# A static planner's urgencies, shifted class by class, in a fused RWKV-6 and MLP kernel

## The chip, the cores and the metric

The kernel runs on one core of one Trainium2 chip. The metric is the device time of one launch in microseconds (us), lower is better. The core has a matrix engine (PE, with its weight loads shown as PEld), a vector engine (DVE), a scalar engine (ACT), a general engine (POOL) and SyncE (SP), which here issues nearly all transfers. Each engine runs its own instructions in the order in which the program lists them.

## The reference

The first half is a linear attention with a decaying state. For each of 4 batches and 8 heads it walks over 768 steps of 48 channels:

```python
for t in range(S):
    cur = np.einsum('bhd,bhe->bhde', u[None] * kt, vt)
    y[:, :, t] = np.einsum('bhd,bhde->bhe', rt, state + cur)
    state = wt[:, :, :, None] * state + np.einsum('bhd,bhe->bhde', kt, vt)
```

The heads are laid side by side (8 x 48 = 384 features), and the second half is a normalised MLP of width 1536 with a residual:

```python
xn = (x - mu) / np.sqrt(var + 1e-06) * g_ln
ch = np.maximum(xn @ w_ch1, 0.0) @ w_ch2
return x + ch
```

## The kernel before

The 4 batches of 768 steps are cut into 8 **rounds** of 384 steps (half a batch each, all 8 heads), numbered 0 to 7. Round 0 is cut again into two **parts**, one of 128 steps and one of 256, so that the first results come early. A part goes through two stages of work.

The first is the scan, `front` (line 1539). Its inputs w, k, r are loaded (`load`, 474; `load_first` in round 0) and turned by PE (`turn`, 502: tiles `w_ps`, `k_ps`, `r_ps`). `totals` (547) multiplies decays pairwise, on DVE or POOL. Then six levels follow one another: `quads` (657) makes 96 small matmuls of 48 rows into a tile `a`, `grow` (689) multiplies k and r by the decays on DVE (tiles `k<-k,tot` and `r<-r,tot` in the profile), and `keep` (718) copies a masked part of the quads into a matrix A on DVE. After them come the transposed k (`kn_ps`), the `states` (860) with a scan on DVE (`s`), and the `outputs` (935). `load_v` (807) fetches v and a half-swapped copy `vx`. `own` makes the term of the current step (tiles `rk`, `vo`), on DVE or POOL.

The second is the MLP: `normalize` (1010) and `turn_x` make the normalised transposed input `xf`; then two products. Rounds 0 to 4 multiply the second product in plain float32 (tiles `o`), and round 0 the first product too (`h_ps<-xf,w`). Round 1 on, the first product is made in three pieces (`hd_ps` and twice `h_ps`), and in rounds 5 to 7 the second product is as well (`thirds`, 1316: nine matmuls for each of 12 slices f of the hidden layer, tiles `a` and `o_2`). The pieces of the weights are made on the way: `convert` (1141) turns 24 fetched blocks of weights into float32 (three ACT and two DVE instructions each), `halve` (1197) and `halve2` (1256) split them.

The small matmuls of `quads`, `states` and `outputs` use parts of the array; the planner calls them `tiled`, and the others not.

**What sets the order.** Nothing above is issued as it is written. Each piece is registered with `plan.add(engine, cost, function, reads, writes, ..., pri=...)`, and `Plan.order` (from line 112 on) then builds the order of every engine once, as the program is built: it keeps a modelled clock for each engine, and picks again and again the engine whose next piece can start first. Among the pieces of that engine that could start within `WAIT[engine]` of the earliest, the one with the lowest urgency number `pri` goes first. A piece that may run on `EITHER` engine (DVE or POOL) goes to the one that can start it first. Constants bend the model:

- `STAY` (in `switching`, 172) is added to the number of a PE piece that would change between tiled and untiled; `DRAIN` is the modelled time of such a change.
- `PATIENCE` (157) is how long, from the time it is ready, a POOL piece marked `port` is held back until DVE runs pieces not so marked.
- `MARGIN` takes the place of `HOP`, the modelled time from one engine to another, for tiled pieces once 60 us have passed (`FILLED`).
- `FETCH` is the modelled interval between fetches of PE's instructions.

Where PE would be idle for over 0.4 us in the first 90 modelled us, matmuls on a constant are put there (lines 192 to 199; tile `idle`).

The number is `at(rnd, stage) = 40 * rnd + stage` (409) for stages 0 to 30 of the scan and the normalisation. Part 0 of round 0 counts as round -1. `CONVERT` is 38. `FILL` is 200, so the MLP of round 0 has 200, of round 1 240, and so on to 320 and 360; rounds 5 to 7 have 400, 440 and 480 plus 2f for slice f, and 3 more for its `thirds`. Copies out of PSUM have `EVICT` = -1000, or a stage less 500.

Two shifts of the diff touch numbers that a reader would not guess: 14 is the fetch of the weights' blocks (`pri - 24`, line 1185; also the fourth `grow` of round 0), and 38 is all the conversions but DVE's share of the first six blocks and the fetches.

Since all pieces are recorded through one helper, every program line in the profile is L49; groups are told apart by their tiles.

Of the kernel before, what the change touches and what calls it, by code (L numbers as in the profile page):

```python
# [1 line left out]

# [63 lines left out]
class Plan:  # L66
# [11 lines left out]

    HOP, MARGIN, FILLED, PATIENCE, STAY = 0.1, 0.1, 60.0, 15.0, 12
    BEFORE, PIECE, FETCH, CROWD = 66, 256, 4.0, 300
    WAITS = 1.006
    DRAIN = {True: 0.1, False: 0.12}
    WAIT = {"PE": 0.1, "DVE": 0.2, "ACT": 0.1, "POOL": 0.05, "SP": 0.05}

    def __init__(self, homes, dynamic):
        self.ops, self.writer, self.readers = [], {}, {}
# [8 lines left out]

    def add(self, eng, cost, fn, r=(), w=(), new=(), pri=0, lat=0.0, size=0, port=None, tiled=False, count=0):
        costs = {eng: cost} if isinstance(eng, str) else dict(zip(eng, cost))
        op = Op(len(self.ops), costs, fn, pri, lat, size, "POOL" in costs if port is None else port, tiled, count)  # L100
        self.ops.append(op)
        for tag, name in new:
            self.tile_tag[name] = tag
            op.new.append((tag, name))
            self.queue[tag].append(op.i)
            self.maker[name] = op.i
        for key in list(r) + list(w):
            if key in self.writer:
                op.need.add(self.writer[key])
            name = key[0] if isinstance(key, tuple) else key  # L110
            op.uses.add(name)
        for tag, name in new:
            op.uses.add(name)
        for key in w:
            op.need.update(self.readers.pop(key, ()))
            self.writer[key] = op.i
        for key in r:
            self.readers.setdefault(key, set()).add(op.i)
        op.uses = {n for n in op.uses if n in self.tile_tag}
        op.need.update(self.maker.get(n, op.i) for n in op.uses)  # L120
        op.need.discard(op.i)
        return op

    def order(self, busy, idle=None, until=0.0):
# [47 lines left out]
        def switching(t, op):  # L172
            drain = self.DRAIN[op.tiled] * (op.tiled != tiled)
            waits = fetches(t + drain, op)[0] > 2 * self.DRAIN[True]
            return self.STAY * (op.tiled != tiled) + self.CROWD * waits

        while todo:
            best = None
            for e, waiting in ready.items():
                at = [(t, op) for op in waiting if (t := start_of(op, e)) is not None]  # L180
                if not at:
                    continue
                first = min(t for t, _ in at)
                t, op = min(
                    ((t, op) for t, op in at if t <= first + self.WAIT[e]),
                    key=lambda x: (x[1].pri + (switching(*x) if e == "PE" else 0), x[1].i),
# [74 lines left out]
def kernel(  # L261
# [673 lines left out]
    def outputs(q, before, part):  # L935
# [49 lines left out]
        for j in range(2):  # L985
            def add(j=j):
                x = tile_("x", x_, [P, TT, H, D])
                y = tiles[y_][:, j, 0 : NK * D].rearrange("p (r c e) -> p r c e", r=NP, c=TT)
                cs = slice(c0, c0 + nc)
                DVE.tensor_tensor(  # L990
                    out=x[:, cs, ts(g, NH)].rearrange("p c (r j) e -> p j r c e", j=2)[:, j],
                    in0=y[:, :, cs],
                    in1=tiles[f"vo{q}"].rearrange("p (r j) c e -> p j r c e", j=2)[:, j, :, cs],
                    op=ALU.add,
                )
            plan.add(
                "DVE", cost(part, 0.12, 0.41), add, r=[y_, (f"vo{q}", c0)], w=[(x_, uu, j, c0)],
                pri=urgent(part, 24),
            )
# [316 lines left out]
    def thirds(rnd, f):  # L1316
# [34 lines left out]
        for i in range(TT):  # L1351
# [49 lines left out]
            if last:  # L1401
                plan.add("DVE", 0.53, add, r=[keys[1]] + whole, w=[(x_, "sum", i)], pri=EVICT)
                plan.add("DVE", 0.53, rest, r=[keys[0], (x_, "sum", i)], w=[(x_, "out", i)], pri=EVICT)
                plan.add("SP", 0.36, store, r=[(x_, "out", i)], pri=EVICT, lat=2.0, size=1.0)
# [27 lines left out]
    def mlp(rnd):  # L1432
# [3 lines left out]
        for f in range(FC):  # L1436
# [39 lines left out]
            def relu(h_=h_):  # L1476
# [13 lines left out]
                w=[ps], new=[("b", ps)], pri=pri - 0.1, lat=0.17,  # L1490
            )
            plan.add("DVE", 0.53, add, r=[ps], w=[h_], pri=EVICT)
            if rnd >= LAST:
                thirds(rnd, f)
# [183 lines left out]
```

## Time and profile before

| what | value |
|---|---|
| median of 3 runs | 539.59 us (535.79 to 541.41) |
| the profiled execution | 537.31 us, its span 535.4 us |
| PE busy, of the span | 521.3 us, 8994 matmuls |
| DVE busy | 403.2 us |
| ACT busy | 269.0 us |
| POOL busy | 73.0 us |
| moved by DMA | 55.84 MB, 104 GB/s on average |

The profile is of one execution. Its span runs from the first to the last instruction, and some 1.9 us of its own time lie around that. Matmuls overlap in the pipeline, so their mean durations (491 ns for an `o` matmul) are longer than the interval at which they follow one another. The chain of waits tells the intervals better, since it cuts the time into pieces without overlap.

### The profile page before, as it was taken

The page shows a single profiled execution, that of the slowest core. Times are in us where ns is not written, and L with a number is a line of the kernel's source. Part 1 is how long each engine was busy: PE and PEld are TensorE (multiplying, and loading weights), DVE is VectorE, ACT ScalarE, POOL GpSimd, SP SyncE. Part 2 cuts the span into 40 slices and gives each one's busy share as a digit, 9 for nine tenths or more (in the row PEclk, how much of TensorE's full clock was granted, in tenths as well). Part 3 has the DMA queues.
Part 4 walks back from the last instruction along what each step waited for, and adds up shares of the span by engine and source line. Part 5 has one row for each costly group of instructions (what it writes and reads, how often), then busy time and mean ns, then how long its engine had stood idle before and what let it go on. Part 6 is the DMA issues. An engine that isn't in the chain of part 4 may idle for free.

```text
span 535.4 us, 20629 instructions
## 1 busy us (share of the span) xinstructions
PE 521.3 (97%) x8994; PEld 434.4 (81%) x8994; DVE 403.2 (75%) x845; ACT 269.0 (50%) x602; POOL 73.0 (14%) x106
## 2 busy tenths in 40 slices
PE   8999899999999999999999999999999999999995
PEld 6778788776989676889766998669867999999994
DVE  6898969797999988999765787546555856656554
ACT  3798868962395532663630885046721434332321
POOL 6212201531203041112110000002200000000000
PEclk9999989999999999999999999999999999999999
DMA  9874864378525646576111415014101322213101
GB/s 222 248 209 142 192 175 105 72 185 237 158 49 105 157 85 131 113 148 146 61 30 37 112 39 139 2 40 115 46 15 60 104 60 88 89 45 108 56 0 45
DMA packets 122362, 55.84 MB, mean 104 GB/s; under 512 B 93984, under 2 KB 119200, under 8 KB 122272
## 3 DMA queue, kind: packets, MB, share of 16 engines
q1 hardware_dynamic: 119152, 53.54, 39.3%
q10 hardware_dynamic: 3120, 0.98, 1.0%
q8 instruction: 71, 1.16, 0.9%
q14 instruction: 19, 0.16, 0.1%
HBM read 45.05 MB, written 7.10 MB: 97 GB/s over the span
## 4 chain that ended last, share of the span: by engine, by line
PE 85%; DVE 7%; DMA 2%; issue 1%; POOL 1%; SPq 1%; ACT 1%; DVEq 0%; POOLq 0%; ACTq 0%
PE a L49 24%; PE o L49 21%; PE h_ps L49 18%; PE hd_ps L49 7%; PE w_ps L49 3%; PE k_ps L49 2%; PE r_ps L49 2%; PE o_2P L49 2%; PE kn_ps L49 2%; DVE x L49 2%; PE xT_ps L49 2%; PE idle L49 1%; DVE k L49 1%; PE o_2D L49 1%; DVE r L49 1%
## 5 line engine op out<-in xcount | busy, mean ns | idle before, releaser
L49 PE MATMUL o<-ffn,h 128*128 128x384 f32 x360 | 124.7, 491 | 0.0
L49 PEld LDWEIGHTS o<-ffn,h 128*128 128x128 f32 x360 | 65.4, 190 | 37.6
L49 PEld LDWEIGHTS a<-r,k 48*60 48x60 f32 (+5 forms) x4608 | 63.1, 126 | 19.6 <-issue 8.5
L49 ACT COPY h<-hd_ps 128x384 f32<-128x384 f32 x84 | 39.9, 479 | 71.6 <-PE hd_ps L49 69.8
L49 DVE SCALAR_TENSOR_TENSOR h<-h_ps,h 128x384 f32<-128x384 f32 x84 | 46.5, 555 | 34.7 <-PE h_ps L49 34.2
L49 PE MATMUL a<-r,k 48*60 48x32 f32 (+5 forms) x4608 | 69.4, 212 | 2.0 <-DVE r L49 1.3
L49 DVE TENSOR_TENSOR k<-k,tot 112x768 f32<-112x768 f32 (+1 forms) x50 | 41.4, 828 | 29.0 <-PE a L49 18.6
L49 PE MATMUL h_ps<-xhl,wl 128*128 128x384 f32 x252 | 60.8, 349 | 0.3
L49 PE MATMUL h_ps<-xhl,wh 128*128 128x384 f32 x252 | 57.9, 338 | 0.0
L49 PE MATMUL hd_ps<-xd,d 128*128 128x384 f32 x252 | 55.4, 347 | 0.0
L49 PEld LDWEIGHTS h_ps<-xhl,wl 128*128 128x128 f32 x252 | 43.7, 188 | 3.5 <-ACT h L49 1.1
L49 PEld LDWEIGHTS h_ps<-xhl,wh 128*128 128x128 f32 x252 | 45.3, 188 | 0.0
L49 PEld LDWEIGHTS hd_ps<-xd,d 128*128 128x128 f32 x252 | 43.9, 188 | 1.1
L49 DVE COPY_PREDICATED A<-mask,a 128x768 f32<-128x768 int8 (+2 forms) x36 | 39.3, 1092 | 0.9 <-PE a L49 0.9
L49 DVE TENSOR_TENSOR r<-r,tot 112x768 f32<-112x768 f32 (+1 forms) x50 | 39.6, 791 | 0.0
L49 ACT ACTIVATE hH<-h 128x384 fp32r<-128x384 f32 x36 | 18.8, 526 | 41.0 <-DVE h L49 41.0
L49 ACT ACTIVATE h<-h 128x384 f32<-128x384 f32 x48 | 25.1, 526 | 20.3 <-DVE h L49 20.1
L49 POOL TENSOR_TENSOR vo<-v,own 128x576 f32<-128x576 f32 (+1 forms) x12 | 13.5, 1121 | 141.3 <-DVE x L49 107.3
L49 ACT COPY w<-w_ps 112x384 f32<-112x384 f32 (+1 forms) x31 | 14.3, 489 | 34.3 <-PE w_ps L49 34.0
L49 DVE SCALAR_TENSOR_TENSOR hL<-h,hH 128x384 fp32r<-128x384 f32 x36 | 20.0, 555 | 14.3 <-ACT hH L49 14.0
L49 ACT COPY A<-a 32x384 f32<-32x384 f32 (+2 forms) x36 | 15.6, 433 | 27.8 <-PE a L49 27.5
L49 PE MATMUL h_ps<-xf,w 128*128 128x128 f32 (+1 forms) x144 | 27.7, 343 | 0.1
(120 smaller groups left out, 1020.3 us busy)
## 6 DMA issues: line engine op xcount, KB each, us to landing
d<-w1d SPq DMA_DIRECT2D x84, 192.0 KB, 2.7
raw<-in_moe_w_ch_dram SPq DMA_DIRECT2D x24, 384.0 KB, 4.3
v<-in_v_dram SPq DMA_DIRECT2D x48, 96.0 KB, 2.8
out_dram<-x SPq DMA_DIRECT2D x24, 192.0 KB, 1.9
nat<-in_w_dram SPq DMA_DIRECT2D x36, 96.0 KB, 3.5
nat<-in_k_dram SPq DMA_DIRECT2D x36, 96.0 KB, 3.2
nat<-in_r_dram SPq DMA_DIRECT2D x36, 96.0 KB, 3.0
w1d<-w1diff SPq DMA_DIRECT2D x12, 192.0 KB, 2.7
```

Of the source, the lines that this page charges most:

```text
L49: ins = self.tc.keep_in_program_order(f(*args, **kw))
```

## The change

Five constants of the planner's model get other values: `MARGIN`, `PATIENCE`, `STAY`, `FETCH` and the table `WAIT`. A table `SHIFTS` is added, and `add` looks up the whole number below a piece's `pri` there and adds what it finds. Numbers of -600 and less (the copies with `EVICT`) are not shifted. Copies with a stage less 500 can be: -232 is the scaled copy of the turned x of round 6, -216 the copy of the turned k of round 7.

All pieces of one class, which share a whole number, are shifted together. No function that issues an instruction is changed, nor its arguments; only the order, the choice between DVE and POOL, the buffer that a tile gets, and the number of `idle` matmuls can come out otherwise.

```diff
-    HOP, MARGIN, FILLED, PATIENCE, STAY = 0.1, 0.1, 60.0, 15.0, 12
-    BEFORE, PIECE, FETCH, CROWD = 66, 256, 4.0, 300
+    HOP, MARGIN, FILLED, PATIENCE, STAY = 0.1, 0.293159, 60.0, 2.0, 2.0
+    BEFORE, PIECE, FETCH, CROWD = 66, 256, 4.11468, 300
     WAITS = 1.006
     DRAIN = {True: 0.1, False: 0.12}
-    WAIT = {"PE": 0.1, "DVE": 0.2, "ACT": 0.1, "POOL": 0.05, "SP": 0.05}
+    WAIT = {"PE": 0.0617605, "ACT": 0.155358, "DVE": 0.170848, "POOL": 0.403865, "SP": 0.0}
+
+    SHIFTS = {
+        -232: 14, -216: -4.5, -38: -42, -37: 5, -33: 10.5, -31: -22, -28: -9, -20: 13, -14: -23,
+        3: -45, 5: -19.5, 10: -35, 12: 4.5, 14: 4, 21: 8, 22: 29.5, 38: 17.5, 51: 68.5, 52: 30,
+        53: -5.5, 54: 24, 55: 4, 58: -30, 62: -4, 63: 26, 66: 2.5, 90: -16, 92: 7.5, 101: -19,
+        104: 56, 121: -39, 127: 29.5, 129: 59.5, 136: -23, 142: 8.5, 160: -5, 169: 47, 176:
+        -27.5, 182: 14, 207: 7.5, 208: 31, 215: -17.5, 246: 0.5, 247: -12.5, 248: 2.5, 249: -35,
+        257: -3.5, 262: 31, 284: 12, 289: 8.5, 306: 4.5, 319: -23.5, 403: 15, 405: 32.5, 409:
+        121.5, 412: -52, 417: 8, 418: -16, 425: -2.5, 445: 2.5, 447: 72, 449: -25, 450: -9.5,
+        451: 14.5, 454: 3.5, 457: 66.5, 459: 88.5, 462: -10, 463: 5, 479: -74, 483: 8.5, 492: 2,
+        493: 22, 497: 64.5, 498: 25.5, 501: 22.5, 502: -8.5,
+    }
...
         costs = {eng: cost} if isinstance(eng, str) else dict(zip(eng, cost))
+        pri += self.SHIFTS.get(math.floor(pri), 0.0) if pri > -600 else 0.0
         op = Op(len(self.ops), costs, fn, pri, lat, size, "POOL" in costs if port is None else port, tiled, count)
```

More of the change, by code (lines that the diff above doesn't have):

```diff
@@ L1 @@
+import math
 from contextlib import ExitStack
```

## The prediction

> **What bounds the kernel now.** I read the page first: which engine is full, and where. PE is at 97% and its row of tenths is 8 or 9 nearly throughout; DVE is as full only in the first half. Of the chain that ended last, PE holds 85%.
>
> ```profile
> PE 521.3 (97%) x8994; PEld 434.4 (81%) x8994; DVE 403.2 (75%) x845; ACT 269.0 (50%) x602; POOL 73.0 (14%) x106
> PE   8999899999999999999999999999999999999995
> DVE  6898969797999988999765787546555856656554
> PEclk9999989999999999999999999999999999999999
> PE 85%; DVE 7%; DMA 2%; issue 1%; POOL 1%; SPq 1%; ACT 1%; DVEq 0%; POOLq 0%; ACTq 0%
> ```
>
> Then the windows by stage (columns: length, busy time of each engine with its count, granted clock, DMA share, GB/s). Between 150 and 427 us PE misses 1.2 us of 277. What an order can win lies before 150 us and at the end; what it can lose can lie anywhere.
>
> ```profile
> 0.00:36.00 36.00, 33.31 (x569) 25.49 (x569) 29.58 (x77) 24.51 (x55) 12.48 (x42) 1.00 0.89 221
> 36.00:150.00 114.00, 110.12 (x2391) 90.08 (x2389) 99.59 (x200) 79.54 (x186) 26.47 (x27) 0.99 0.63 159
> 150.00:300.00 150.00, 149.18 (x3741) 118.83 (x3740) 127.24 (x259) 70.20 (x160) 26.53 (x30) 1.00 0.44 98
> 300.00:427.00 127.00, 126.59 (x1731) 102.25 (x1731) 82.36 (x191) 60.80 (x136) 7.50 (x7) 1.00 0.23 67
> 427.00:536.00 109.00, 102.06 (x570) 97.77 (x568) 64.39 (x122) 33.94 (x69) 0.00 (x0) 0.99 0.19 60
> ```
>
> A busy PE isn't always useful. PE's groups by shape show matmuls on a constant, 9.0 + 3.0 + 1.1 = 13.1 us, and the tile's own view puts all of them in the first 33 us: the start is emptier than its 33.31 of 36 says.
>
> ```profile
> L49 PE MATMUL idle<-nought 128*128 128x384 f32 x20 | 9.0, 556 | 1.0 <-DVE eps L49 1.0
> L49 PE MATMUL idle<-nought 128*128 128x256 f32 x8 | 3.0, 458 | 0.0
> L49 PE MATMUL idle<-nought 128*128 128x128 f32 x6 | 1.1, 272 | 0.0
> ```
>
> PE's waits (total, times, longest) name one large stall and a few small ones.
>
> ```profile
> PE k_ps L49 <- DMA nat<-in_k_dram: 2.3, 1, 2.3
> PE a L49 <- DVE r L49: 1.3, 3, 0.6
> ...
> PE a L49 <- DVE hD L49: 0.7, 2, 0.4
> ```
>
> The chain in order of time (start, length) gives that load, the price of changing between tiled and untiled matmuls, and the tail. 42 `o` matmuls in a row took 13.55 us, 0.3226 each, so 12 need 3.87; between two blocks of quads they took 4.07. That is 0.20 us of change, and some 0.1 more on the small matmuls' side.
>
> ```profile
> 62.63 4.93 DMA nat<-in_k_dram
> 287.23 4.07 PE o L49 x12
> 393.83 13.55 PE o L49 x42
> 531.99 0.56 DVE x L49
> ```
>
> **The change, part by part.** It adds and removes no arithmetic; only the `idle` matmuls can differ in number. Matmuls, loads and copies cost what they cost; a gain is PE time that isn't useful now, a loss is new such time. On the profiled execution the movable part is: idle matmuls 13.1; the load's stall; the other named waits, 1.3 + 0.7 + 0.5 + 0.4 + 0.3 + 0.3 = 3.5; and the tail, from PE's last end at 530.2 (timeline) to 535.4, 5.2.
>
> *1. Part 0 (shifts from -38 to -14) and the early classes up to 38.* They move r's first load and the normalisation ahead, part 0's first quads back, turns of part 1 (3, 5) ahead, and put the states of round 0 (22) 29.5 later. PE wins only where DVE feeds it sooner, and DVE is idle 36 - 29.6 = 6.4 us in the first 36: that bounds the gain, and as much may be lost. The nearest row is the chain at 22.6 to 24.5 us, where three pieces of weight conversion on DVE (0.75, 0.84, 0.07) stand ahead of the scan `s`. Taking these 1.7 away and about as much elsewhere: -3.
>
> *2. The late load.* The k load issued at 62.63 landed at 67.56, and PE turned it at 67.69, 2.3 us after its previous matmul's end. The cost is larger than that, as the clock shows:
>
> ```profile
> 65.00:67.60 2.60, 0.40 (x3) 0.15 (x2) 2.46 (x6) 0.84 (x2) 0.00 (x0) 1.00 0.77 143
> 67.60:69.50 1.90, 1.73 (x10) 1.52 (x11) 1.90 (x2) 0.57 (x2) 0.00 (x0) 0.80 0.75 166
> 69.50:72.20 2.70, 2.70 (x9) 2.04 (x8) 0.56 (x1) 1.19 (x4) 0.00 (x0) 0.51 1.07 307
> ```
>
> At a clock of 0.80 and then 0.51, 1.9 x 0.20 + 2.7 x 0.49 = 1.7 us were lost behind the gap: 4.0 in all. [...] The trace says 4.0, and I use it, for a gap made anew too. Ahead of that load, the chain has SP issuing two swapped copies and weight fetches (pieces of 0.60 and 0.61 us). Fetches go from 14 to 18, behind v (16) and its swap (17) of round 0; conversions go from 38 to 55.5, behind round 1's first levels, which frees DVE for round 1. The load itself (number 81) isn't shifted and waits for a buffer that the scan releases, so it comes sooner if the scan does. Gone: -4.0; the same gap elsewhere: 0; twice: +4.0. I take -2.5, more likely gone than not.
>
> *3. The other waits.* `STAY` from 12 to 2 and `MARGIN` from 0.1 to 0.29 have PE turn to other ready work instead of a tiled piece that is only just due. Of 3.5 us I take -1.5; the bounds are -3.5 and, for each new wait of the sort, +0.5.
>
> *4. Changes of tiling.* PE's timeline has 86 blocks of tiled matmuls. Counting the calls, the program registers 60 quads, 18 states and 18 outputs, 96 pieces, so nearly every piece is its own block already. A freer `STAY` can add at most 10 blocks, 10 x 0.3 = +3.0; moving states and outputs together can take some away, say 10, -3.0. I take 0.
>
> *5. The end (403 to 502).* Slices of `thirds` are put far back (409 by 121.5, 447 by 72, 457 and 459 by 66 and 88): a stock of ready matmuls, nine of 0.175 = 1.6 us each, for when the last h pieces pass through DVE, ACT, DVE, DVE. There the weight load waits 0.68 and 0.70 for `hD`; 1.4 can be covered. The tail has six DVE additions from 529.22 to 532.55; with only the last two behind PE's end, it would be 1.1 shorter. Bound -2.5, or +1.6 if one more slice is left over for the end; I take -1.4.
>
> *6. `PATIENCE` from 15 to 2, `WAIT` of POOL to 0.40.* POOL will sooner take `rk`, `vo` or `tot` while DVE is in full use. The rows: a POOL `rk` takes 1.41, a DVE one 0.75, and a DVE conversion beside POOL took 1.21 at 64.09 where its neighbours took 0.56, so 0.65 lost. But over 36 to 300 us, with 57 POOL pieces of 53 us, k's multiplication means 999 ns against r's 951, 1.7 us over all 35: POOL hardly disturbs DVE. [...] In 36 to 300 DVE has 264 - 226.8 = 37 us idle that would hide most of it. I take +0.4, with -1 and +6 as ends.
>
> Sum: -3 - 2.5 - 1.5 + 0 - 1.4 + 0.4 = -8.0. From 537.31 that gives 529.3; the median shown lies 2.3 above the profiled execution, which would give 531.6.
>
> **The rivals.** *A: gaps only move.* PE is at 99% for 277 us and the start is bound by loads (DMA share 0.89) and DVE; a shift acts only where two pieces are ready together. Then steps 1 and 2 bring nothing and the rest is 1 to 3: some 537. This is also the case in which the table hardly does what it says, its classes winning no tie. Against: 26 us of movable time, most of it early, where many classes compete.
>
> *B, slower: conversions come too late.* At 55.5, 18 of the 24 blocks stand behind round 1's levels on ACT and DVE. By DVE's groups their share is 12 x (0.352 + 0.663) + 6 x (0.42 + 0.55) = 18.0 us, and DVE's idle time from 36 to 150 us is 14.4. Round 0's first product and all later filling wait for these weights. If they aren't done when PE has used up what else it has, about 70 us, PE stands idle between quads, each gap paying the clock as in step 2: two such gaps, +8.0, without the gains, near 547. For: DVE at 87% in that window. Against: list order still lets a ready conversion run whenever round 1 waits for PE.
>
> **How the numbers follow.** Forecast, -8: 0.56, its own range 524 to 535. A: 0.28, 535 to 540. B, or POOL in the way as in step 6: 0.16, 540 to 550. What one can tell from no change is about 1%, 5.4 us, so faster is under 534.2 and slower above 545. Nearly all of the forecast's case is faster, and a little of it isn't: faster 0.54, within 1% 0.33, slower 0.13. Predicted time 531.5. The range leaves out under a tenth of the chance at each end: 522, with steps 1, 2 and 5 near their bounds, to 543, which takes in A and the mild half of B.
>
> **What would show it.** Step 1: idle matmuls well under 13.1 us. Step 2: no wait of PE for a load of k, and a granted clock of 1.00 between 60 and 75 us. Step 3: waits of `a` for DVE below 1.3. Step 4: 86 blocks, give or take 10. Step 5: no wait for `hD` near the end, and under 5.2 us behind PE's last matmul. Step 6: POOL's count above 106 and the mean of `k<-k,tot` near 1000 ns. I am wrong if PE's idle time between 36 and 150 us grows past 3.9, or if a new wait appears in the 277 us that are full now.

## The result, and the profile after

The changed kernel takes 530.49 us, the median of 4 runs (528.18 to 531.5), against 539.65 (535.79 to 541.41) before: ratio 0.984, with a 95% interval from 0.9802 to 0.9878. The forecast was 531.5. The profiled execution took 528.18 us, with a span of 526.2, so 9.2 less than the 535.4 before.

That the total fits doesn't mean that the steps do. The page of the changed kernel first: the totals, PE's tenths, and the chain by engine.

```profile
PE 514.0 (98%) x8984; PEld 434.7 (83%) x8984; DVE 398.5 (76%) x839; ACT 268.4 (51%) x602; POOL 82.4 (16%) x112
PE   8999799999999999999999999999999999999996
...
PE 93%; DVE 3%; POOL 1%; issue 1%; DMA 1%; ACT 0%; DVEq 0%; POOLq 0%
```

PE's part of the chain rose from 85% to 93%. The fifth slice, about 60 us, is worse than it was (7, where it was 8); what was gained lies elsewhere. The idle matmuls, from PE's groups by shape, are 6.7 + 2.4 + 0.8 = 9.9 us, where they were 13.1, and the last of them now stands at 52 us:

```profile
L50 PE MATMUL idle<-nought 128*128 128x384 f32 x14 | 6.7, 573 | 1.0 <-DVE eps L50 1.0
L50 PE MATMUL idle<-nought 128*128 128x256 f32 x6 | 2.4, 482 | 0.0
L50 PE MATMUL idle<-nought 128*128 128x128 f32 x4 | 0.8, 272 | 0.0
```

PE's waits (total, times, longest) name as much as before, 7.9 us in all against 7.7, with other names:

```profile
PE a L50 <- issue: 1.7, 2, 1.2
PE k_ps L50 <- DMA nat<-in_k_dram: 1.6, 2, 1.3
...
PE a L50 <- DVE r L50: 0.8, 1, 0.8
PE k_ps L50 <- ACT w L50: 0.6, 1, 0.6
```

A late load of k is still there, and so is a lower clock behind it (length, busy time of each engine, clock, DMA share, GB/s):

```profile
64.00:67.00 3.00, 1.49 (x7) 0.68 (x5) 2.23 (x6) 0.38 (x1) 0.00 (x0) 1.00 0.97 255
67.00:69.50 2.50, 2.37 (x15) 2.37 (x16) 0.00 (x0) 1.53 (x4) 0.00 (x0) 0.69 0.91 201
69.50:72.20 2.70, 2.57 (x16) 2.20 (x16) 2.54 (x4) 1.01 (x4) 0.00 (x0) 0.65 0.71 219
```

It is not the same load, though. Round 2 loads its k in two halves of three transfers each. In the kernel before they were issued at 62.63 and 68.70 us, and PE waited for the first half. In the changed kernel SP (SPq is its queue; start, length, transfers) issues the first half at 49.09, and PE turns it at 53.83 with no wait that the table names; now it waits for the second half:

```profile
49.09 2.80 SPq L50 DMA_DIRECT2D nat<-in_k_dram  x3
62.82 1.49 SPq L50 DMA_DIRECT2D nat<-in_k_dram  x3
```

```profile
66.16 0.61 PE L50 MATMUL k_ps<-ident,nat 128*112 128x128 f32 x2 [1.29 <-DMA nat<-in_k_dram]
```

Two gains show elsewhere, which the prediction had put at 0 and at 1.4 us. Counted along PE's timeline, there are 74 blocks of tiled matmuls in place of 86. And the last 100 us have no wait of PE that the table names.

### The profile page after: what moved, and what is told of

Same layout as the page of the kernel before. It is cut to its first block, busy times and chain, and to the rows that moved or that the text cites. A ratio compares the mean times of both kernels' runs of the same rounds, so it can differ in the third digit from the quotient of the medians.

```text
span 526.2 us, 20613 instructions
## 1 busy us (share of the span) xinstructions
PE 514.0 (98%) x8984; PEld 434.7 (83%) x8984; DVE 398.5 (76%) x839; ACT 268.4 (51%) x602; POOL 82.4 (16%) x112
## 4 chain that ended last, share of the span: by engine, by line
PE 93%; DVE 3%; POOL 1%; issue 1%; DMA 1%; ACT 0%; DVEq 0%; POOLq 0%
PE a L50 25%; PE o L50 22%; PE h_ps L50 21%; PE hd_ps L50 9%; PE r_ps L50 3%; PE k_ps L50 3%; PE w_ps L50 3%; PE o_2P L50 2%; PE kn_ps L50 2%; PE xT_ps L50 1%; PE idle L50 1%; PE o_2D L50 1%; DMA nat<-in_k_dram 1%; DVE k L50 1%; POOL rk L50 1%
## 5 line engine op out<-in xcount | busy, mean ns | idle before, releaser
L50 PEld LDWEIGHTS a<-r,k 48*63 48x63 f32 (+5 forms) x4608 | 63.4, 126 | 15.6 <-issue 7.5
L50 PE MATMUL a<-r,k 48*63 48x32 f32 (+5 forms) x4608 | 69.5, 212 | 2.7 <-issue 1.7
L50 PE MATMUL h_ps<-xhl,wl 128*128 128x384 f32 x252 | 59.7, 345 | 0.0
L50 PE MATMUL hd_ps<-xd,d 128*128 128x384 f32 x252 | 56.5, 349 | 0.0
L50 DVE TENSOR_TENSOR k<-k,tot 112x768 f32<-112x768 f32 (+1 forms) x50 | 40.3, 807 | 8.4 <-PE a L50 5.9
L50 POOL TENSOR_TENSOR rk<-nat,nat 128x576 f32<-128x576 f32 (+1 forms) x13 | 17.8, 1372 | 65.9 <-DVE ffn L50 20.9
L50 DVE TENSOR_TENSOR x<-o,x 128x384 f32<-128x384 f32 x15 | 8.3, 554 | 25.1 <-PE o L50 25.1
L50 ACT COPY A<-a 32x384 f32<-32x384 f32 (+2 forms) x36 | 15.5, 432 | 19.4 <-PE a L50 19.1
```

Of the source, the lines that this page charges most:

```text
L50: ins = self.tc.keep_in_program_order(f(*args, **kw))
```

## The experiments

Ratios are to the kernel before, run on the same chip, with the 95% interval. In the diffs, the shifts kept are named by their range. Theory 1 is the prediction's own: PE's losses are separate, and each class of shifts wins its own. Theory 4 was formed after the first four runs: the shifts and the constants are one set, and taking any part out meets an order that the rest was not made for.

**The end alone, and all but the end.**

```diff
-    constants and SHIFTS of the changed kernel
+    constants of before; SHIFTS: 403 to 502 alone
```

> The kernel before with only the shifts from 403 to 502 (the MLP of rounds 5 to 7), old constants; 86 tiled blocks and the idle matmuls stay as before. Theory 1 (the time is the sum of PE's separate losses, each won where its own classes are): the last 110 us lose their small waits and the tail gets 1 us shorter, together 4 to 5 us, ratio 0.991 to 0.993, and nothing changes before 400 us. Theory 2 (the gain lies in the scan, with fewer changes of tiling and a better start; the end is cover only): ratio 0.998 to 1.0. Theory 3 (the new constants make the gain): 1.0.

```diff
-    SHIFTS of the changed kernel
+    SHIFTS: -232 to 319 alone
```

> The changed kernel without the shifts from 403 to 502; 74 tiled blocks as in the changed kernel. Theory 1: it gives back 4 to 5 us, ratio to the kernel before 0.991 to 0.994, with waits for hD and hH back at the end. Theory 2: as the changed kernel, 0.983 to 0.986. Theory 3: the same, 0.983 to 0.986.

All but the end: 0.9941 (0.9915 to 0.9968), so the end is worth about 1% to the changed kernel, as theory 1 said. In the profiles the spans are 531.2 and 526.2, 5.0 apart. But the end alone gave 1.0028 (1.0006 to 1.005): slightly slower. None of the three theories expects both. PE's timeline of that kernel shows why (start, length, matmul, idle time before it):

```profile
435.96 0.69 PE L50 MATMUL hd_ps<-xd,d 128*128 128x384 f32 x3
437.99 0.44 PE L50 MATMUL a<-w2d,hD 128*128 128x384 f32 x1 [1.34 <-DVE hD L50]
```

That wait and another for `hD` at 452 us are 3.0 us in total, and with a lower clock (0.97 in the window below) they eat what the end gains elsewhere. PE's matmuls come in the same order as before up to about 420 us; from the matmul at which the orders part, the rest of the span is 117.6 us here and 116.8 in the kernel before.

**The constants alone, and the shifts alone.**

```diff
-    SHIFTS of the changed kernel
+    SHIFTS = {}
```

> The five new constants, no shifts; 87 tiled blocks (before: 86, changed: 74). Theory 1: no blocks saved and no end gained, only what the start wins, 0 to 3 us, ratio 0.995 to 1.0, or above 1 where the old urgencies don't fit the new constants. Theory 2: 1.0. Theory 3: 0.983 to 0.988.

```diff
-    constants of the changed kernel
+    constants of before
```

> All shifts with the old constants; 83 tiled blocks, and 61 arithmetic pieces on POOL in place of 70. Theory 1: the end's 4 to 5 us and 3 blocks at 0.25, ratio 0.989 to 0.992. Theory 2: without the fewer blocks little is left, 0.996 to 1.0. Theory 3: 0.996 to 1.0.

The constants alone: 1.0209 (1.0169 to 1.0248). The shifts alone: 1.0356 (1.0315 to 1.0397). Either half of the change makes the kernel slower, and both together make it faster. All three theories fell here (theory 1 had left room for a slower kernel with the constants alone, but not with the shifts alone). The waits of PE with the constants alone:

```profile
PE a L50 <- DVE A L50: 3.1, 1, 3.1
PE hd_ps L50 <- DMA d<-w1d: 3.0, 1, 3.0
PE r_ps L50 <- DMA nat<-in_r_dram: 1.5, 2, 0.8
PE r_ps L50 <- DVE h L50: 1.3, 1, 1.3
```

and with the shifts alone:

```profile
PE a L50 <- DVE r L50: 4.6, 2, 4.4
PE a L50 <- DVE hD L50: 3.0, 2, 1.7
```

Each is a few long waits. The longest of each kernel, 3.1 and 4.4 us, turn out below to have the same cause.

**The end with its own constants.** The order stays that of before up to 400 us of the planner's clock:

```diff
+    LATE = {"PE": 0.0617605, "ACT": 0.155358, "DVE": 0.170848, "POOL": 0.403865, "SP": 0.0}
+    def wait(self, free):
+        return self.LATE if free["PE"] > 400.0 else self.WAIT
...
-                    ((t, op) for t, op in at if t <= first + self.WAIT[e]),
+                    ((t, op) for t, op in at if t <= first + self.wait(free)[e]),
-                after = max(now, after) + self.FETCH
+                after = max(now, after) + (4.11468 if free["PE"] > 400.0 else self.FETCH)
```

> The kernel before up to 400 modelled us; from there the new WAIT and FETCH, and the shifts from 403 to 502. 86 tiled blocks. Theory 4 (the shifts repair an order that the new constants make; each needs the other): the two waits for hD of 1.5 and 1.8 us that the shifts alone had near 436 and 452 us are gone, and the last 110 us gain what they gain in the changed kernel, 4 to 5 us: ratio 0.990 to 0.993. Rival (the gain at the end needs the earlier order, which leaves other work over for it): the waits for hD stay, ratio 0.998 to 1.004.

0.9922 (0.9899 to 0.9944): with two of the constants beside them, `WAIT` and `FETCH`, the same shifts win 4.2 us on the old order. Counted from the matmul at which the orders part, the rest of the span is 112.8 us against 117.9 before, 5.1 less; by the same count the end is worth 4.8 us to the changed kernel (113.2, and 118.0 without it). The window from 430 to 455 us (PE's busy time and matmuls come first) of the end alone, then of this run, then of the kernel before, then of the changed one:

```profile
430.00:455.00 25.00, 21.60 (x118) 20.66 (x119) 11.19 (x24) 7.57 (x17) 0.00 (x0) 0.97 0.19 56
```

```profile
430.00:455.00 25.00, 25.00 (x147) 24.90 (x146) 16.72 (x34) 8.08 (x17) 0.00 (x0) 1.00 0.22 66
```

```profile
430.00:455.00 25.00, 24.92 (x140) 23.69 (x140) 15.01 (x28) 9.29 (x20) 0.00 (x0) 1.00 0.26 77
```

```profile
430.00:455.00 25.00, 25.00 (x147) 24.92 (x146) 16.92 (x32) 9.14 (x19) 0.00 (x0) 1.00 0.25 79
```

The end alone left PE idle for 3.4 us of these 25; the other three are full, and the two with end shifts and new constants have PE always busy, also in its weight loads (24.90 and 24.92, against 23.69 before). For the end, then, the rival falls, and theory 4 holds in part: the shifts of the end need their constants, but with them they win as much on the old order as on the new one, as theory 1 has it. `WAIT` and `FETCH` alone don't decide it, though: two later runs have the same pair of waits with the new constants.

**The price of a change of tiling.** 42 of the quads get one more float32 product of zeros, which the trace shows as two matmuls of 128 columns. It writes columns that the quads then overwrite. Nothing of it is known to the planner, so the order stays that of the changed kernel. Once it stands ahead of the quads, where PE usually was untiled anyhow, and once between the two halves:

```diff
             to = tiles[name].rearrange("s j (u r c t) -> s j u r c t", u=U, r=NP, t=C // 2)
+            if rnd:                      # ahead of the quads
+                PE.matmul(
+                    tiles[name][:, 0, 256:384], zeros, nought.broadcast_to([P, P]),
+                    start=True, stop=True,
+                )
             for uu in us:
+                if rnd and uu:           # or here, between their halves
+                    PE.matmul(
+                        tiles[name][:, 0, 256:384], zeros, nought.broadcast_to([P, P]),
+                        start=True, stop=True,
+                    )
```

> The changed kernel with one more untiled 128-column matmul of zeros ahead of each of 42 quads, into columns that the quads overwrite. 84 tiled blocks in place of 74. If a change there and back costs 0.25 us: 42 x 0.11 + 10 x 0.25 = 7 us, ratio to the kernel before 0.997. If changes cost nothing: 4.6 us, 0.993.

> The same 42 matmuls of zeros, each now between the two halves of its quads, so that it breaks the block: 116 tiled blocks. If a change there and back costs 0.25 to 0.30 us, it is 32 x 0.25 to 0.30 = 8 to 10 us slower than with the matmuls ahead, ratio to the kernel before 1.012 to 1.015. If changes cost nothing, or other work hides them: as with the matmuls ahead, 0.993 to 0.997.

Ahead: 1.0179 (1.0137 to 1.022), 549.59 us. Inside: 1.0319 (1.0277 to 1.0361), 556.63 us. Both are slower than expected; as the matmuls are two, not one, they cost 42 x 2 x 0.109 = 9.2 us by themselves. PE's timeline of the second run shows one broken block:

```profile
154.67 0.62 PE L50 MATMUL a<-r,k 48*32 48x32 f32 x48
155.22 0.49 PE L50 MATMUL a<-nought 128*128 128x128 f32 x2
155.64 0.62 PE L50 MATMUL a<-r,k 48*32 48x32 f32 x48
```

From 155.22 to 155.64 are 0.42 us for two matmuls that follow one another in 0.109 elsewhere. Over the 42 breaks, the medians between starts are 0.144 from the last small matmul to the first of zeros (0.007 among small ones), 0.213 to the second (0.109), and 0.205 to the next small one (0.109): 0.137 + 0.104 + 0.096 = 0.337 us for a change there and back. That makes the second run 9.2 + 42 x 0.337 = 23.4 us slower than the changed kernel, and its named waits are 10.7 us in all, 2.8 longer; 26.2, and 556.63 - 530.49 is 26.1. So the price is paid in full, and no other work hides it. (The profiled executions, from which the waits are taken, have spans 29.3 us apart: that of the changed kernel is the fastest of its four. The sum is good to some 3 us.)

The first run should have cost 9.2 + 10 x 0.337 = 12.6 and cost 19.1. Its named waits are 14.6 us in all, 6.7 longer than in the changed kernel, which gives 19.3. The longest are

```profile
PE a L50 <- issue: 9.6, 7, 2.4
```

7.9 more than in the changed kernel; some other waits are shorter. These waits lie inside the quads, and are taken up in the last section.

**The start taken out.**

```diff
-    SHIFTS of the changed kernel
+    SHIFTS: those from -38 to 38 left out
```

> The changed kernel without the shifts from -38 to 38 (round 0 and the conversions). 85 tiled blocks, and as many idle groups as in the changed kernel. Theory 1 (parts add up): the start gives back its 3 us and 11 blocks give back 2.8, ratio to the kernel before 0.994 to 0.996. Theory 4 (each needs the other): later shifts meet an order that they were not made for and large single waits appear, ratio above 1.0.

1.0053 (1.0033 to 1.0072). The idle matmuls came back (36 of 14.2 us, where as many as in the changed kernel, 24, were expected), and so did 11 blocks, 3.7 us at 0.337. The largest single loss is a wait at 216 us, some 120 us behind the last of the conversions, whose shifts were taken out (PE's timeline):

```profile
214.84 1.44 PE L50 MATMUL a<-r,k 48*56 48x32 f32 x96
221.27 2.02 PE L50 MATMUL a<-r,k 48*62 48x32 f32 x65 [5.00 <-DVE r L50]
```

With the clock behind it (0.50 from 219.6 to 226.4 us, another 3.4 us lost), this is most of the 12.1 us that the run is slower than the changed kernel. The name of the wait, DVE, is not its cause. DVE itself had stood still until just before, for a load of r (DVE's timeline):

```profile
217.20 0.76 DVE L50 TENSOR_TENSOR rk<-nat,nat 128x576 f32<-128x576 f32 x1 [5.55 <-DMA nat<-in_r_dram]
```

`rk`, the first piece of `own`, needs r as it was loaded. The planner put it on DVE, ahead of the growing of k and r that the quads wait for, and its load landed at 217.12. Theory 4's number came, then, and theory 1's blocks are part of it.

**One constant, or one class, at a time.** `PATIENCE` back to 15, `STAY` back to 12; then 81 shifted by -71; then the last 6 of the weights' 24 fetches put back by 70:

```diff
-    HOP, MARGIN, FILLED, PATIENCE, STAY = 0.1, 0.293159, 60.0, 2.0, 2.0
+    HOP, MARGIN, FILLED, PATIENCE, STAY = 0.1, 0.293159, 60.0, 15.0, 2.0
```

> The changed kernel with PATIENCE 15 again; 83 tiled blocks in place of 74, and POOL takes 58 arithmetic pieces in place of 76. Theory 1 (parts add up): 9 blocks at 0.337 us, the price that the matmuls of zeros measured, are 3.0; 18 pieces more on DVE, where some of it is hidden, 0 to 5: ratio to the kernel before 0.990 to 0.999. Theory 4 (each value needs the others): single waits of PE over 2 us beyond the load of k, ratio over 1.0.

```diff
-    HOP, MARGIN, FILLED, PATIENCE, STAY = 0.1, 0.293159, 60.0, 2.0, 2.0
+    HOP, MARGIN, FILLED, PATIENCE, STAY = 0.1, 0.293159, 60.0, 2.0, 12
```

> The changed kernel with STAY 12 again; the order is the same up to some 120 us, then 79 tiled blocks in place of 74. Theory 1: 5 x 0.337 = 1.7 us, ratio to the kernel before 0.986 to 0.989. Theory 4: a wait over 2 us appears between 120 and 400 us, ratio over 0.992.

```diff
+        ... 81: -71,
```

> The changed kernel with one more shift, 81 by -71: the loads of round 2's k stand ahead of what else SP could issue. SP now issues one load of r ahead of a swapped copy of v; 74 tiled blocks. If the order of SP is what makes PE wait for k near 64 us: that wait and the lower clock behind it go, up to 3 us, ratio to the kernel before 0.977 to 0.981. If the buffer or the traffic sets when k lands (DMA engines busy 0.9 and more from 53 to 69 us): no gain there, 0.983 to 0.990.

```diff
-        plan.add("SP", 0.4, fetch, w=[raw_], new=[("raw", raw_)], pri=pri - 24, lat=2.0, size=1.05)
+        plan.add("SP", 0.4, fetch, w=[raw_], new=[("raw", raw_)], pri=pri - 24 + 70 * (i >= 18), lat=2.0, size=1.05)
```

> The changed kernel with the last 6 of 24 blocks of weights fetched 70 later in urgency, behind the loads of round 2, 2.4 MB less traffic ahead of them; 79 tiled blocks. SP's order is the same until some 75 us, so the wait for k near 64 us must stay; then the order moves. Theory 1: 5 blocks at 0.337, 1.7 us, ratio to the kernel before 0.986 to 0.990. Theory 4: a large wait appears later, over 0.992.

`PATIENCE` 15: 1.0284 (1.023 to 1.0338). `STAY` 12: 1.0053 (1.0013 to 1.0093). The k load: 0.9863 (0.9819 to 0.9907), which can't be told from the changed kernel. The late weights: 1.0299 (1.0259 to 1.0339). Three of the four are theory 4's numbers. With `STAY` 12, where the blocks explain 1.7 us of some 11, PE's waits between 195 and 275 us begin with

```profile
PE a L50 <- DVE r L50: 3.3, 2, 2.9
PE xT_ps L50 <- DVE h L50: 2.4, 1, 2.4
```

The stretch from 200 to 275 us tells which runs are slower, though not by how much. Windows of the changed kernel, of the kernel before, and of the one with no start:

```profile
200.00:275.00 75.00, 74.51 (x1977) 62.66 (x1977) 67.42 (x141) 38.24 (x87) 14.09 (x15) 1.00 0.52 114
```

```profile
200.00:275.00 75.00, 74.18 (x1786) 60.28 (x1786) 66.61 (x131) 37.21 (x84) 14.31 (x16) 1.00 0.50 112
```

```profile
200.00:275.00 75.00, 68.90 (x1753) 56.27 (x1754) 60.79 (x126) 32.81 (x76) 13.09 (x14) 0.95 0.46 100
```

| kernel | ratio | PE busy, 200 to 275 us | longest named wait of PE there | DVE idle ahead of an `rk` there |
|---|---|---|---|---|
| changed | 0.984 | 74.51, clock 1.00 | 0.3 | none |
| before | 1 | 74.18, clock 1.00 | 0.6 | none |
| constants alone | 1.0209 | 69.54, clock 0.98 | 3.1, DVE A | 5.33 |
| shifts alone | 1.0356 | 69.35, clock 0.95 | 4.4, DVE r | 5.21 |
| no start | 1.0053 | 68.90, clock 0.95 | 5.0, DVE r | 5.55 |
| `PATIENCE` 15 | 1.0284 | 71.56, clock 0.95 | 3.0, DVE r | 5.26 |
| `STAY` 12 | 1.0053 | 68.62, clock 0.95 | 2.9, DVE r | 4.19 |
| late weights | 1.0299 | 71.23, clock 0.95 | 3.2, DVE r | 3.73 |

Six partial versions have a wait of about 3 to 5 us of PE for DVE there, and a lower clock around it. The last column (DVE's timelines) shows that it is one misfit and not six: in each, an `rk` on DVE starts within 0.3 us of the landing of its load of r, and PE's wait ends 3 to 5 us behind that. In the other runs no `rk` holds DVE up for even 1 us. The changed kernel has a load of r that lands as late (226.23 us), but there POOL takes the `rk`, at 226.52, and DVE goes on; in the kernel before POOL waits 3.96 us for its load and PE doesn't notice:

```profile
226.52 1.44 POOL L50 TENSOR_TENSOR rk<-nat,nat 128x576 f32<-128x576 f32 x1 [0.78 <-DVE s L50]
```

```profile
207.57 1.41 POOL L49 TENSOR_TENSOR rk<-nat,nat 128x576 f32<-128x576 f32 x1 [3.96 <-DMA nat<-in_r_dram]
```

No run moves this piece alone, so how much of each wait it makes is not measured. Nor was a rival to theory 4 tested: that a kept order is the one that escapes such a misfit, and that changes taken at random would bring it back as often as the parts taken out here.

The k load wasn't moved by its shift: its second half was issued at 63.02 us (62.82 in the changed kernel), SP only issued a load of r earlier, and PE's waits for k are 2.1 us, where they were 1.6. Whether its buffer or the traffic sets the time of landing stays open; the six late fetches came too late in the order to tell. `PATIENCE` 15 and the late weights have two waits for `hD` of 1.3 and 1.7 us near 451 and 467 us too, with the new constants. What decides between the two forms of the end stays open as well.

No version beat the changed kernel.

## Why the prediction was right, and where its steps were not

The total, -8 from the profiled execution, became -9.2 in the span. By the starts of PE's matmuls, the losses changed thus: idle matmuls -3.0, changes of tiling -3.9, everything behind 420 us -4.9, pauses elsewhere +2.0. That is -9.8; the other 0.6 lie in small differences. When they were won is another matter. Taking each useful matmul that PE had begun at the interval at which its kind usually follows itself, the changed kernel was ahead by 0.2 us at 75 us, 1.2 at 150, 1.8 at 300 and 4.4 at 420 (estimates from the starts in the two timelines). So the first 75 us, where steps 1 and 2 had put -5.5, brought almost nothing.

*Step 1, the start: the sign came, the gain didn't.* -3 was predicted, and the windows of the idle matmuls add up to 12.24 us before and 9.28 after. But at 75 us PE had begun 1414 useful matmuls where it had begun 1407 before: 12 turns more, and 5 matmuls fewer of round 0's first product, worth about 0.2 us. Pauses took the place of the filler: between 36 and 60 us PE is idle for 1.4 us, where it was 0.3. The step that failed is to count filler as lost time that comes back when the filler goes. (Without the classes up to 38 the idle matmuls are back, and so they are with `PATIENCE` 15: it takes both to be rid of them.)

*Step 2, the late load: failed.* "I take -2.5, more likely gone than not." The load that step 2 read, the first half of round 2's k, did come sooner, by 13.5 us, and PE's wait for it is gone. But PE also came sooner to the second half, and waits for that, 1.29 and 0.36 us: "the same gap elsewhere: 0", which the step had named. Between 60 and 75 us PE is busy for 11.64 us where it was 12.04. The clock's part of the step held: 0.69 and 0.65 over 2.5 and 2.7 us cost 0.8 + 0.9 = 1.7 us again. In the 7.9 us ahead of that (60.00 to 67.90) PE was busy for 4.67 us and no gap was longer than 1.29.

*Step 3, the other waits: failed.* Of -1.5, nothing came. Without the load of k and the two at the start, the named waits are 4.5 us, where they were 3.5. The kind that the step argued from, waits of `a` for DVE, did fall, from 2.4 to 1.4. But the largest now, 1.7, is of the kind `issue`, behind nothing that the profile shows: the step had 0.5 of it in its sum, and weighed nothing that could make it grow.

*Step 4, changes of tiling: mis-sized, and the largest miss.* It had counted the blocks rightly and named 10 fewer, -3.0, as a bound, but set that against as many more and took 0. 12 blocks fewer at 0.337 us are 4.0 us. By PE's timelines it is states and outputs that come to stand beside quads, in 9 blocks where it was 3. Neither half of the change does it: 87 blocks with the constants alone, 83 with the shifts alone, 74 with both. The price was taken a little low, at 0.3.

*Step 5, the end: mis-sized.* The mechanism was right as far as it went: no wait for `hD` is left, and behind PE's last matmul (timelines of PE and of DVE) the tail is 526.2 - 522.04 = 4.2 us, from 5.2.

```profile
521.71 0.33 PE L50 MATMUL o_2P<-w2h,hH 128*128 128x384 f32 x1
```

```profile
522.74 0.56 DVE L50 SCALAR_TENSOR_TENSOR x<-o_2P,x 128x384 f32<-128x384 f32 x1
```

But -1.4 counted named waits and the tail. The whole is some 5 us on either order. The difference is in pauses too short for a name: in the window from 430 to 455 us PE was busy for 24.92 of 25 us before and its weight loads for 23.69, against 25.00 and 24.92 in the changed kernel. The table of waits holds nothing of that.

*Step 6, POOL: right that little is lost.* POOL takes 112 pieces in place of 106, and still disturbs DVE less: k's multiplication (DVE's groups by shape) is at

```profile
L50 DVE TENSOR_TENSOR k<-k,tot 112x768 f32<-112x768 f32 x35 | 33.4, 954 | 7.6 <-PE a L50 5.4 <-issue 2.0
```

954 ns, no longer 999 (the mean of the whole run, which the prediction gave to 36 to 300 us; there alone it is 1006). In the kernel before 5 of the 35 ran beside a POOL piece, and two of them took 1.88 and 1.53 us; in the changed kernel none did, and the longest took 0.98. A piece of r did there, at 177.71 us, and took 1.12, where the mean of its form is 0.95. So this order mostly keeps these pieces apart. No run shows the step's +0.4 by itself, nor its end of +6: what the runs showed is DVE busy for 398.5 us in place of 403.2, with POOL busy for 82.4 in place of 73.0.

*The rivals.* Half of A came: steps 1 and 2 brought almost nothing, as it says, but the rest brought 9 us and not 1 to 3. B didn't come: DVE is busy for 98.79 us between 36 and 150, 99.59 before, and PE stands idle between quads for no longer than 1.23 us. But the prediction's own sign of being wrong did appear: PE's idle time from 36 to 150 us grew from 3.9 to 4.8. PE with nothing to do between quads, as in B, is what six partial versions show, at 216 us and later and not at 70, and there DVE isn't full: it waits for a load.

The reasoning underneath was the weakest part. It summed steps as if each class won its own gain. The runs show that it isn't so: the constants cost 2.1% and the shifts 3.6%, each alone. A right total from six terms of which three failed and two were mis-sized is luck in good part: the 4 us of steps 2 and 3 that didn't come and 2 us of new pauses were made up by some 7 us, of tiling and of the end, that weren't foreseen.

## What to carry to other kernels

Where a planner builds the order, judge its constants and its urgencies as one set: here a part of the set mostly did not bring a part of the gain (the end, with its own constants, did). Ask of a wait for an engine whether that engine was at work or itself waiting; behind six waits "for DVE" here DVE itself had waited for a load. For an engine that is 97% busy, look at what its busy time holds: changes of mode and pauses too short for a name brought nearly all of the gain here, while the named waits were 7.7 us in all before and 7.9 after. Less filler was no gain by itself here (3.2 us less of it, some 0.2 us ahead at 75 us): count the useful work begun by a given time. The price of a change of mode is best measured by breaking blocks on purpose, with the same extra work beside them as a control.

## What the hardware showed that was not expected

**PE stops with nothing named, at regular counts of its instructions, where these are short.** In the changed kernel one block of quads stops for 1.23 us in its middle, released by nothing that the profile shows:

```profile
60.35 1.39 PE L50 MATMUL a<-r,k 48*60 48x32 f32 x82 [0.78 <-DVE r L50]
62.97 0.41 PE L50 MATMUL a<-r,k 48*60 48x32 f32 x14 [1.23 <-issue]
```

That is 127 matmuls behind the other such stop of this kernel, of 0.44 us at 56.72. With the matmuls of zeros ahead, five such stops come between 195 and 306 us. Counted in matmuls on PE, they are 638, 254, 637 and 1021 apart, which is 5, 2, 5 and 8 times 127.5, or 255 instructions with the weight loads. With the zeros inside, they come at the same five matmuls, and two earlier stops of the first run, at 60 and 67 us, come at the same two matmuls as those of the changed kernel. In all 14 runs every such stop (over 0.25 us) comes in tiled matmuls or at most four wide ones behind them. The page of the changed kernel has this queue:

```profile
q8 instruction: 70, 1.15, 0.9%
```

If this queue is PE's, 70 packets for its 2 x 8984 instructions are 257 for each, of 16 KB. That PE waits at these stops for the next packet of its own instructions is an estimate of the author's, from the two counts, 255 and 257: no run shows which engine the queue serves, nor what ends a stop. It would fit the places: 128 wide matmuls at the 0.175 us of those in `thirds` last 22 us, and a block of 96 quads 1.44 (at 214.84 us with no start). With 84 matmuls that the planner doesn't know of, five more stops came in the quads, 6.6 us in the first run and 2.7 in the second, and the two earlier ones, present in the changed kernel too, were 1.4 us longer in the first and gone in the second. So in the first run the added matmuls cost nearly as much by such stops (6.6 + 1.4 = 8.0 us) as by their own time (9.2).

**The clock fell behind single gaps of 2.30 and 1.29 us, and stayed at 1.00 behind one of 2.45.** By the loads of k the granted clock was 0.50 for 3.41 us, in the kernel before and in the changed one alike; the wider windows above mix this with a clock of 1.00:

```profile
68.75:72.16 3.41, 3.41 (x13) 2.75 (x12) 1.31 (x1) 1.71 (x5) 0.00 (x0) 0.50 1.05 291
```

```profile
67.96:71.37 3.41, 3.28 (x17) 2.91 (x16) 1.77 (x3) 1.63 (x6) 0.00 (x0) 0.50 0.86 227
```

That is 1.7 us lost each time. In the 8 or 9 us ahead of it PE was idle for 3.0 and 3.2 us in all, and the longest single gaps were 2.30 and 1.29. With `STAY` 12 a wait of 2.45 us at 274 us left the clock at 1.00 (window from 250 to 300). So the length of one gap doesn't tell; what does is not shown by these runs. In the kernel with no start, the 75 us that hold the wait of 5.0 us have a mean of 0.95.
